# Loading i_gate and x in 4 KB runs, with word transposes of norm and gated input, GpSimd writing with a stride of two bf16

## Chip, cores, metric

One core of one Trainium2 chip. The metric is the device time of one execution in microseconds (us). A run counts as slow when it is over 1.5% above the fastest run of the same kernel; ratios use the other runs alone. The clock named here is the share of its full clock that PE was granted, as the trace records it. ACT is ScalarE, DVE is VectorE, POOL is GpSimd, PE is TensorE, SP issues the loads and stores. Medians and ratios below are of the runs named beside them.

## The reference, cut to what matters

Four sequences of 6336 tokens with 256 channels. A gated linear recurrence feeds a small gated unit:

```python
log_a = 8.0 * sigmoid(r_gate) * log(clip(sigmoid(a_param), 1e-6, 1 - 1e-6))
a_t = exp(log_a)
norm = sqrt(maximum(1.0 - a_t * a_t, 1e-6))
x_gated = norm * sigmoid(i_gate) * x
h = a_t[:, t] * h + x_gated[:, t]          # for each token t; y[:, t] = h
# then: gate = sigmoid(causal 5-tap convolution of y), out = (gate * (y @ w_val)) @ w_out
```

## The kernel before

Tokens pass in 28 chunks of up to 1024, split into 51 tiles of up to 512. The recurrence wants channels on the partitions, the loads bring tokens there, so PE transposes much. PSUM is the memory that PE writes its results to; a bank is a part of it. Each tile goes through these steps: load of r_gate, i_gate and x; `tanh` of both gates in one ACT instruction; `u2` = (tanh(i)+1)·x on DVE or POOL, as a string of letters says; `srT`, transpose of tanh(r); `exp`; `e` = a² on POOL; `sq` (square root on ACT, several chunks at once); `nT`, transpose of the norm back to tokens; `xg` = norm·u2 on DVE; `xT`, transpose of that to channels; `scan` on DVE; then `conv` (the convolution, PE), `tg` (tanh of it, ACT), `val` (y @ w_val, PE), `gv` (the gated value, DVE), `out` (times w_out, PE), `osb` (its copy out of PSUM, DVE or ACT) and `store`. Tiles in the traces are named by what holds them: `gp` is the result of conv, `bank` that of any transpose or of out.

The program is unrolled. A planner in the kernel (list scheduling) reads a table of costs and priorities, and emits every step in the order in which its model starts them. It also assigns PSUM banks that way. COST and PRIO do nothing else; OSB and U2 choose engines:

```python
OSB = "ADDDDDDDDDDDDADDD..."        # which engine copies each piece out of PSUM
U2 = "PDPDDDDDDPDPDPDPDDPDPPPP..."  # u2 of each tile on DVE (D, 15 tiles) or POOL (P, 36)
COST = dict(load=(0.05, 2.8), loadx=(0.02, 1.5), ..., u2P=(0.25, 3.15), u2D=(0.2, 1.55), ..., scan=(0.21, 2.14), ...,
            store=(0.05, 1.3))      # fixed part and part per tile or chunk, us
PRIO = dict(load=5.92, loadx=5.97, ...)
# ... make_plan: of all steps that could go next, take the one with the earliest start, ties by PRIO ...
order.sort(key=lambda o: o[0])
```

The parts that the change touches:

```python
# load: r_gate in 4 KB runs (a partition gets nj = 4 tokens in a row), i_gate and x in 1 KB runs
nc.sync.dma_start(ri[:, 0, 0:nw, 0:nj, :], rf[t0:t0 + nt, :].rearrange("(w p j) d -> p w j d", w=nw, j=nj))
nc.sync.dma_start(ri[:, 1, 0:nw, 0:nj, :]..., if_[t0:t0 + nt, :].rearrange("(k p) d -> p k d", p=P))
# u2
if eng == "DVE":
    nc.vector.scalar_tensor_tensor(out=u, in0=ti, scalar=1.0, in1=xt, op0=ALU.add, op1=ALU.mult)
else:
    nc.gpsimd.tensor_scalar(out=t1, in0=ti, scalar1=1.0, scalar2=1.0, op0=ALU.mult, op1=ALU.add)
    nc.gpsimd.tensor_tensor(out=u, in0=t1, in1=xt, op=ALU.mult)
# nT and xT: one bf16 transpose of 128x128 for each 128 tokens and 128 channels
nc.tensor.transpose(out=nT[:, j, h * P:(h + 1) * P], in_=nring[:, h, n0 + j * P:n0 + (j + 1) * P], identity=ident_b[:])
```

The output weight `wo` comes by a DMA from POOL's queue, and DVE halves it:

```python
nc.vector.tensor_scalar(out=wo[:], in0=wo[:], scalar1=0.5, scalar2=None, op0=ALU.mult)
```

Of the kernel before, what the change touches and what calls it, by code (L numbers as in the profile page):

```python
# [9 lines left out]
P = 128  # L10
WIN = 512
CHUNK = 1024
SUB = WIN // P
# [8 lines left out]
NU = 10  # L22
NY = 6
NIN = 2
NX = 3
NTR = 3
NTI = 5
# [7 lines left out]

U2 = "PDPDDDDDDPDPDPDPDDPDPPPPPPPPPPPPPPPDPPPPPPPDPPPPPPP"

COST = dict(load=(0.05, 2.8), loadx=(0.02, 1.5), tanh=(0.2, 1.7), u2P=(0.25, 3.15), u2D=(0.2, 1.55), srT=(0.05, 0.45), exp=(0.35, 0.86), e=(0.1, 1.8),
            sq=(0.3, 1.71), nT=(0.05, 0.47), xg=(0.1, 0.58), xT=(0.05, 0.45), scan=(0.21, 2.14), conv=(0.2, 1.1), tg=(0.19, 0.83),
            val=(0.02, 0.93), gv=(0.15, 1.07), out=(0.02, 0.47), osbD=(0.68, 0), osbA=(0.59, 0),  # L40
            store=(0.05, 1.3))
PRIO = dict(load=5.92, loadx=5.97, store=2.53, tanh=6, exp=2.8, sq=0.42, tg=-0.32, srT=-1.6, nT=0.31, xT=3.79,
            conv=5.3, val=4.34, out=2.99, e=5.93, u2=6, xg=4.55, scan=0.36, gv=-0.61, osb=-0.99)
TABLE, SEM, DMA_LAT = 1.3, 0.15, 2.2
# [1 line left out]
FP32 = mybir.dt.float32  # L46
BF16 = mybir.dt.bfloat16
ACT = mybir.ActivationFunctionType
ALU = mybir.AluOpType
# [60 lines left out]
def make_jobs(sh):  # L110
# [8 lines left out]
    def job(op, eng, f, deps, cost=None, bank=0):  # L119
        fix, per = COST[cost or op]  # L120
        jobs[op].append((eng, fix + per * f, [d for d in deps if d[1] >= 0], bank))
# [31 lines left out]
    for u, n in enumerate(UNITS):  # L153
        size = sum(sh.chunks[c][1] for c in range(ends[u] - n, ends[u])) / CHUNK
        fix, per = COST["sq"]
        jobs["sq"].append(("ACT", fix * len(sh.runs[u]) + per * size, [("e", 2 * ends[u] - 1)], 0))
# [57 lines left out]
def kernel(  # L214
# [11 lines left out]
    nc = tc.nc  # L226
    B, S, D = x.shape
# [3 lines left out]
    xf = x.rearrange("b s d -> (b s) d")  # L231
    rf = r_gate.rearrange("b s d -> (b s) d")
    if_ = i_gate.rearrange("b s d -> (b s) d")
    of = out.rearrange("b s d -> (b s) d")

    shape = Shape(B * S, S)
    tiles, chunks, chunk_of, pieces = shape.tiles, shape.chunks, shape.chunk_of, shape.pieces
    plan, banks = make_plan(shape)

    const = ctx.enter_context(tc.tile_pool(name="const", bufs=1))  # L240
    inp = ctx.enter_context(tc.tile_pool(name="inp", bufs=3))
    live = {}

    def load(c):
        t0, nt, g0, g1 = chunks[c]
        nw, nj = g1 - g0, nt // (g1 - g0) // P
        ri = inp.tile([P, 2, 2, SUB, D], FP32, name="ri", tag="ri", bufs=NIN)

        nc.sync.dma_start(ri[:, 0, 0:nw, 0:nj, :], rf[t0:t0 + nt, :].rearrange("(w p j) d -> p w j d", w=nw, j=nj))
        nc.sync.dma_start(ri[:, 1, 0:nw, 0:nj, :].rearrange("p w j d -> p (w j) d"),  # L250
                          if_[t0:t0 + nt, :].rearrange("(k p) d -> p k d", p=P))
        live["ri", c] = ri

    def loadx(c):
        t0, nt, g0, g1 = chunks[c]
        xt = inp.tile([P, 2 * SUB, D], FP32, name="xt", tag="xt", bufs=NX)
        nc.sync.dma_start(xt[:, 0:nt // P, :], xf[t0:t0 + nt, :].rearrange("(k p) d -> p k d", p=P))
        live["xt", c] = xt

    with tc.manual_schedule():  # L260
# [9 lines left out]
        ident_f = const.tile([P, P], FP32, name="ident_f")  # L270
        make_identity(nc, ident_f[:])
        ident_b = const.tile([P, P], BF16, name="ident_b")
# [15 lines left out]
        with tc.tile_pool(name="ps_setup", bufs=1, space=bass.MemoryType.PSUM) as ps_setup:  # L288
# [9 lines left out]
                                    op0=ALU.max, op1=ALU.min)  # L298
# [5 lines left out]
            for h in range(H):  # L304
                nc.tensor.transpose(out=wc_ps[:, h, :], in_=wrow[0:CONV_K, h * P:(h + 1) * P],
                                    identity=ident_f[0:CONV_K, 0:CONV_K])
# [8 lines left out]
        rings = ctx.enter_context(tc.tile_pool(name="rings", bufs=1))  # L315
        work = ctx.enter_context(tc.tile_pool(name="work", bufs=2))
        psum = ctx.enter_context(tc.tile_pool(name="psum", bufs=1, space=bass.MemoryType.PSUM))
        def bank(b, dtype):
            return psum.tile([P, WIN * 4 // mybir.dt.size(dtype)], dtype, name=f"bank{b}", tag=f"bank{b}", bufs=1)

        aring = rings.tile([P, H, NS * WIN], FP32, name="aring")
        ering = rings.tile([P, H, NE * WIN], FP32, name="ering")
        nring = ering[:].bitcast(BF16)
        tring = rings.tile([P, NTR + NTI, SUB, D], BF16, name="tring")
        uring = rings.tile([P, NU, SUB, D], BF16, name="uring")
        yring = rings.tile([P, H, NY * WIN], BF16, name="yring")

        def transposes(dst, srcs, h):
            col = 0
            for src, nj in srcs:  # L330
                for j in range(nj):
                    nc.tensor.transpose(out=dst[:, col:col + P], in_=src[:, j, h * P:(h + 1) * P],  # L332
                                        identity=ident_b[:])
                    col += P

        def op_load(g, eng):
            if ("load", g) not in before:
                load(g)
# [5 lines left out]
        def op_tanh(g, eng):  # L344
            nj = tiles[g][1] // P
            c = chunk_of[g]
            ri, w = live["ri", c], g - chunks[c][2]
            if g == chunks[c][3] - 1:
                del live["ri", c]
            r, i = g % NTR, NTR + g % NTI  # L350
            nc.scalar.activation(out=tring[:, r:i + 1:i - r, 0:nj, :], in_=ri[:, :, w, 0:nj, :], func=ACT.Tanh, scale=0.5)  # L351

        def op_u2(g, eng):
            nj = tiles[g][1] // P
            c = chunk_of[g]
            w = g - chunks[c][2]
            xt, ti = live["xt", c][:, w * nj:(w + 1) * nj, :], tring[:, NTR + g % NTI, 0:nj, :]
            u = uring[:, g % NU, 0:nj, :]
            if eng == "DVE":
                nc.vector.scalar_tensor_tensor(out=u, in0=ti, scalar=1.0, in1=xt, op0=ALU.add, op1=ALU.mult)  # L360
                return
            t1 = work.tile([P, SUB, D], FP32, name="t1", tag="t1", bufs=1)[:, 0:nj, :]
            nc.gpsimd.tensor_scalar(out=t1, in0=ti, scalar1=1.0, scalar2=1.0, op0=ALU.mult, op1=ALU.add)  # L363
            nc.gpsimd.tensor_tensor(out=u, in0=t1, in1=xt, op=ALU.mult)  # L364

        def op_srT(k, eng):
            c, h = k // 2, k % 2
            srT = bank(banks["srT", k], BF16)
            transposes(srT, [(tring[:, g % NTR], tiles[g][1] // P) for g in range(*chunks[c][2:])], h)
            live["srT", k] = srT  # L370

        def op_exp(k, eng):
# [17 lines left out]

        def op_nT(g, eng):
            c = chunk_of[g]
            n0, nt = shape.npos[c] + tiles[g][0] - chunks[c][0], tiles[g][1]
            nT = bank(banks["nT", g], BF16)[:].rearrange("p (j d) -> p j d", d=D)
            for h in range(H):
                for j in range(nt // P):
                    nc.tensor.transpose(out=nT[:, j, h * P:(h + 1) * P],  # L397
                                        in_=nring[:, h, n0 + j * P:n0 + (j + 1) * P], identity=ident_b[:])
            live["nT", g] = nT

        def op_xg(g, eng):
            nj = tiles[g][1] // P
            u = uring[:, g % NU, 0:nj, :]
            nc.vector.tensor_tensor(out=u, in0=live.pop(("nT", g))[:, 0:nj, :], in1=u, op=ALU.mult)  # L404

        def op_xT(k, eng):
            c, h = k // 2, k % 2
            xT = bank(banks["xT", k], BF16)
            transposes(xT, [(uring[:, g % NU], tiles[g][1] // P) for g in range(*chunks[c][2:])], h)
            live["xT", k] = xT  # L410

        def yend(c):
            return shape.ypos[c - 1] + chunks[c - 1][1] if c else 0
# [4 lines left out]
        def op_scan(k, eng):  # L418
            c, h = k // 2, k % 2
            t0, nt, g0, g1 = chunks[c]  # L420
            a0, y0 = shape.apos[c], shape.ypos[c]
            yp = yend(c) - 1
            xT = live.pop(("xT", k))
            for (c0, c1, fresh) in shape.segments(t0, nt):
                nc.vector.tensor_tensor_scan(  # L425
                    out=yring[:, h, y0 + c0:y0 + c1], data0=aring[:, h, a0 + c0:a0 + c1], data1=xT[:, c0:c1],
                    initial=0.0 if fresh else yring[:, h, yp:yp + 1], op0=ALU.mult, op1=ALU.add)
# [55 lines left out]
        def op_out(q, eng):  # L483
            g, i = pieces[q]
            gv = live["gv", g]
            ops = bank(banks["out", q], FP32)
            for e in range(2):
                for hk in range(H):
                    nc.tensor.matmul(out=ops[:, e * D:(e + 1) * D], lhsT=gv[:, 2 * i + e, hk, :], rhs=wo[:, hk, :],  # L489
                                     start=(hk == 0), stop=(hk == H - 1))  # L490
            live["ops", q] = ops
# [12 lines left out]
        def op_store(g, eng):  # L504
# [6 lines left out]
                           nT=op_nT, xg=op_xg, xT=op_xT, scan=op_scan, conv=op_conv, tg=op_tg, val=op_val, gv=op_gv,  # L511
                           out=op_out, osb=op_osb, store=op_store)
# [32 lines left out]
```

## Time and profile before

| before | |
|---|---|
| time, median of 2 | 320.17 us (317.40 and 322.94) |
| span of the profiled run, clock | 317.1 us, 0.973 |
| ACT busy / idle | 290.1 / 27.0 us |
| DVE, POOL busy | 270.4, 224.6 us |
| main DMA queue | 91.8% of the span, 291 us |

"Busy" is the sum of an engine's instructions in the span; idle is the span less that. The prediction below prints the lines of the busy table, the slices, the stretches and the waits.

### The profile page before, as it was taken

The numbers are of one execution on the slowest core, as the hardware profiler recorded it, in microseconds if no ns is written. First come the engines' busy times: TensorE is split into PE (matmuls) and PEld (weight loads), VectorE is DVE, ScalarE is ACT, GpSimd is POOL, SyncE is SP. The second block draws the span as 40 slices with busy tenths as digits, with TensorE's granted clock in tenths as the row PEclk, the third lists the DMA queues.
The fourth block names the chain that finished last, engine by engine and source line by source line (L and its number), as shares of the span: only waits on it lengthen the run. The fifth ranks groups of instructions, "written<-read, shape, count | busy, mean of one in ns | idle before, by whom it ended". The sixth has DMA issues, their size and how long they took to land.

```text
span 317.1 us, 7227 instructions
## 1 busy us (share of the span) xinstructions
PE 246.2 (78%) x2987; PEld 163.6 (52%) x2987; DVE 270.4 (85%) x269; ACT 290.1 (91%) x231; POOL 224.6 (71%) x140
## 2 busy tenths in 40 slices
PE   1262877687679768897989798959977997999994
PEld 1141745453546446564655375627644665655662
DVE  3125799999597998999999999997998999999892
ACT  6789999899969999999998999899989999998963
POOL 6329551869469536999989999999997289868000
PEclk9999999999759999999999999997999999999997
DMA  8999999999999999999999999996999994853334
GB/s 208 340 365 380 367 368 382 386 345 352 394 322 349 389 356 375 350 391 385 357 382 382 393 369 383 393 389 191 395 385 383 385 379 164 262 189 133 135 154 179
DMA packets 67327, 104.55 MB, mean 330 GB/s; under 512 B 3287, under 2 KB 54238, under 8 KB 67294
## 3 DMA queue, kind: packets, MB, share of 16 engines
q1 hardware_dynamic: 65904, 103.82, 91.8%
q0 software_dynamic: 1376, 0.26, 1.0%
q8 instruction: 23, 0.38, 0.5%
q14 instruction: 10, 0.08, 0.1%
q10 hardware_dynamic: 14, 0.01, 0.0%
HBM read 78.39 MB, written 25.95 MB: 329 GB/s over the span
## 4 chain that ended last, share of the span: by engine, by line
ACT 25%; DMA 23%; DVE 21%; PE 13%; issue 10%; POOL 4%; SPq 1%; DVEq 0%; ACTq 0%; POOLq 0%
DMA ri<-in_i_gate_dram 15%; DVE yring L425 9%; ACT tring L351 8%; DMA xt<-in_x_dram 6%; DVE gv L477 5%; ACT ering L388 5%; PE bank L489 4%; ACT tg L459 4%; ACT aring L376 4%; PE gp L451 3%; DVE osb L500 3%; PE bank L397 3%; POOL uring L364 2%; DMA ri<-in_r_gate_dram 2%; DVE uring L404 2%
## 5 line engine op out<-in xcount | busy, mean ns | idle before, releaser
L384 POOL TENSOR_TENSOR ering<-aring 128x1024 f32<-128x1024 f32 (+2 forms) x56 | 97.1, 1753 | 55.0 <-ACT aring L376 52.8
L425 DVE TENSOR_TENSOR_SCAN yring<-aring,yring,bank 128x1024 bf16<-128x1024 f32 (+5 forms) x54 | 110.1, 2052 | 0.7 <-PE bank L332 0.5
L351 ACT ACTIVATE tring<-ri 128x2048 bf16<-128x2048 f32 (+1 forms) x51 | 93.9, 1868 | 7.8 <-DMA ri<-in_i_gate_dram 7.7
L364 POOL TENSOR_TENSOR uring<-t,xt 128x1024 bf16<-128x1024 f32 (+1 forms) x36 | 83.6, 2323 | 9.9 <-DMA xt<-in_x_dram 7.3
L451 PE MATMUL gp<-yring,diag 64*64 64x512 bf16 (+14 forms) x1196 | 67.9, 350 | 6.7 <-ACT tg L459 4.6
L489 PE MATMUL bank<-wo,gv 128*128 128x256 bf16 x396 | 57.3, 279 | 18.5 <-DVE gv L477 8.2
L477 DVE SCALAR_TENSOR_TENSOR gv<-tg,val 128x1024 bf16<-128x1024 bf16 (+1 forms) x54 | 60.3, 1120 | 6.7 <-ACT tg L459 4.5
L376 ACT ACTIVATE aring<-bank,khf 128x1024 f32<-128x1024 bf16 (+2 forms) x56 | 59.6, 1111 | 3.3 <-PE bank L332 2.5
L459 ACT ACTIVATE tg<-gp 128x1024 bf16<-128x1024 f32 (+1 forms) x51 | 51.1, 1003 | 7.1 <-PE gp L451 6.8
L489 PEld LDWEIGHTS <-gv 128*128 128x128 bf16 x396 | 36.0, 99 | 37.9 <-issue 16.4
L467 PE MATMUL val<-yring,wv 128*128 128x512 bf16 (+1 forms) x204 | 51.5, 376 | 0.8 <-DVE gv L477 0.8
L500 DVE COPY osb<-bank 128x512 f32<-128x512 f32 x69 | 45.6, 679 | 3.8 <-PE bank L489 3.3
L451 PEld LDWEIGHTS <-diag 64*64 64x64 bf16 x1196 | 30.9, 108 | 33.0 <-issue 16.5
L388 ACT ACTIVATE ering<-ering,b 128x2048 bf16<-128x2048 f32 (+4 forms) x15 | 46.7, 3112 | 0.3
L332 PE MATMUL bank<-ident_b,tring 128*128 128x128 bf16 x396 | 31.3, 231 | 18.5 <-ACT tring L351 13.0
L397 PE MATMUL bank<-ident_b,ering 128*128 128x128 bf16 x396 | 32.9, 240 | 15.8 <-ACT ering L388 12.5
L404 DVE TENSOR_TENSOR uring<-bank,uring 128x1024 bf16<-128x1024 bf16 (+1 forms) x51 | 33.4, 669 | 11.8 <-PE bank L397 11.6
L363 POOL TENSOR_SCALAR t<-tring 128x1024 f32<-128x1024 bf16 (+1 forms) x36 | 40.1, 1115 | 2.6 <-ACT tring L351 1.2
L397 PEld LDWEIGHTS <-ering 128*128 128x128 bf16 x396 | 28.1, 108 | 23.3 <-ACT ering L388 15.5
L332 PEld LDWEIGHTS <-tring 128*128 128x128 bf16 x396 | 25.7, 103 | 27.7 <-ACT tring L351 15.1
L332 PE MATMUL bank<-ident_b,uring 128*128 128x128 bf16 x396 | 30.4, 226 | 3.3 <-DVE yring L425 1.8
L360 DVE SCALAR_TENSOR_TENSOR uring<-tring,xt 128x1024 bf16<-128x1024 bf16 x15 | 24.4, 1624 | 8.2 <-DMA xt<-in_x_dram 8.2
(32 smaller groups left out, 112.6 us busy)
## 6 DMA issues: line engine op xcount, KB each, us to landing
out_dram<-osb SPq DMA_DIRECT2D x48, 512.0 KB, 7.1
ri<-in_r_gate_dram SPq DMA_DIRECT2D x23, 1024.0 KB, 8.1
ri<-in_i_gate_dram SPq DMA_DIRECT2D x23, 1024.0 KB, 11.8
xt<-in_x_dram SPq DMA_DIRECT2D x23, 1024.0 KB, 10.7
ri<-in_r_gate_dram SPq DMA_DIRECT2D x2, 512.0 KB, 5.9
ri<-in_i_gate_dram SPq DMA_DIRECT2D x2, 512.0 KB, 8.1
xt<-in_x_dram SPq DMA_DIRECT2D x2, 512.0 KB, 8.1
ri<-in_r_gate_dram SPq DMA_DIRECT2D x3, 256.0 KB, 2.9
```

Of the source, the lines that this page charges most:

```text
L332: nc.tensor.transpose(out=dst[:, col:col + P], in_=src[:, j, h * P:(h + 1) * P], identity=ident_b[:])
L351: nc.scalar.activation(out=tring[:, r:i + 1:i - r, 0:nj, :], in_=ri[:, :, w, 0:nj, :], func=ACT.Tanh, scale=0.5)
L364: nc.gpsimd.tensor_tensor(out=u, in0=t1, in1=xt, op=ALU.mult)
L376: nc.scalar.activation(out=aring[:, h, a0:a0 + nt].rearrange("c (w p j) -> c w p j", p=P, j=nj), in_=live.pop(("srT", k))[:, 0:nt].rearran ...
L384: nc.gpsimd.tensor_tensor(out=ering[:, h, e0:e0 + nt], in0=a, in1=a, op=ALU.mult)
L388: nc.scalar.activation(out=nring[:, :, 2 * e0:2 * e0 + m], in_=ering[:, :, e0:e0 + m], func=ACT.Sqrt, scale=-0.25, bias=b025[:, 0:1])
L397: nc.tensor.transpose(out=nT[:, j, h * P:(h + 1) * P], in_=nring[:, h, n0 + j * P:n0 + (j + 1) * P], identity=ident_b[:])
L425: nc.vector.tensor_tensor_scan(out=yring[:, h, y0 + c0:y0 + c1], data0=aring[:, h, a0 + c0:a0 + c1], data1=xT[:, c0:c1], initial=0.0 if fr ...
L451: nc.tensor.matmul(out=gp[64 * h:64 * h + 64, m, c0:c1], lhsT=diag[rows, h, kk, rows], rhs=yring[rows, h, src:src + c1 - c0], start=(sh == 0),
L459: nc.scalar.activation(out=tg[:, :, 0:nt], in_=live.pop(("gp", g))[:, :, 0:nt], func=ACT.Tanh, scale=0.5)
L477: nc.vector.scalar_tensor_tensor(out=gv[:, 0:nj, hs, :].rearrange("c j h p -> c j (h p)"), in0=tg[:, hs, 0:nt].rearrange("c h (p j) -> c j ...
L489: nc.tensor.matmul(out=ops[:, e * D:(e + 1) * D], lhsT=gv[:, 2 * i + e, hk, :], rhs=wo[:, hk, :], start=(hk == 0), stop=(hk == H - 1))
```

## The change

Its intent: i_gate and x also in 4 KB runs, to make the DMA work lighter. Then a partition holds four tokens in a row, and two adjacent tokens of a channel have to end up side by side for the scan. So u2 is stored as pairs of bf16, and norm and gated input are transposed as 32-bit words, half as many transposes. GpSimd reads in order and writes every second bf16; DVE reads with a stride, writes in order, and needs two instructions for it.

```diff
-COST = dict(load=(0.05, 2.8), loadx=(0.02, 1.5), tanh=(0.2, 1.7), u2P=(0.25, 3.15), u2D=(0.2, 1.55), ...
-            store=(0.05, 1.3))
+COST = dict(load=(0.05, 2.72), loadx=(0.02, 1.37), tanh=(0.2, 1.7), u2P=(0.25, 3.4), u2D=(0.3, 1.75), ...
+            store=(0.05, 1.33))
...
+    def by_token(src, c):
+        t0, nt, g0, g1 = chunks[c]
+        return src[t0:t0 + nt, :].rearrange("(w p j) d -> p w j d", w=g1 - g0, p=P)
...
+        nc.sync.dma_start(ri[:, 0:nw, 0, 0:nj, :], by_token(rf, c))
+        nc.sync.dma_start(ri[:, 0:nw, 1, 0:nj, :], by_token(if_, c))
...
+        nc.sync.dma_start(xt[:, 0:nw, 0:nj, :], by_token(xf, c))
...
+                tk = ti.rearrange("p (w e) d -> p w d e", e=2)
+                for k in range(nj // 2):
+                    nc.vector.scalar_tensor_tensor(out=u[:, k], in0=tk[:, k], scalar=1.0, in1=xt[:, k], op0=ALU.add,
+                                                   op1=ALU.mult)
...
-            nc.gpsimd.tensor_tensor(out=u, in0=t1, in1=xt, op=ALU.mult)
+            nc.gpsimd.tensor_tensor(out=u.rearrange("p w d e -> p w e d"), in0=t1.rearrange("p (w e) d -> p w e d", e=2),
+                                    in1=xt.rearrange("p w d e -> p w e d"), op=ALU.mult)
...
+                    nc.tensor.transpose(out=nT[:, w * D + h * P:w * D + (h + 1) * P],
+                                        in_=ering[:, h, n0 + w:n0 + nw * P:nw], identity=ident_f[:])
...
+                    nc.tensor.transpose(out=xT[:, at + w:at + nw * P:nw],
+                                        in_=uring_w[:, g % NU, w * D + h * P:w * D + (h + 1) * P], identity=ident_f[:])
```

OSB, U2, PRIO and the sizes of the rings are left as they were.

More of the change, by code (lines that the diff above doesn't have):

```diff
@@ L36 @@
 U2 = "PDPDDDDDDPDPDPDPDDPDPPPPPPPPPPPPPPPDPPPPPPPDPPPPPPP"
-COST = dict(load=(0.05, 2.8), loadx=(0.02, 1.5), tanh=(0.2, 1.7), u2P=(0.25, 3.15), u2D=(0.2, 1.55), srT=(0.05, 0.45), exp=(0.35, 0.86), e=(0.1, 1.8),
+COST = dict(load=(0.05, 2.72), loadx=(0.02, 1.37), tanh=(0.2, 1.7), u2P=(0.25, 3.4), u2D=(0.3, 1.75), srT=(0.05, 0.45), exp=(0.35, 0.86), e=(0.1, 1.8),
             sq=(0.3, 1.71), nT=(0.05, 0.47), xg=(0.1, 0.58), xT=(0.05, 0.45), scan=(0.21, 2.14), conv=(0.2, 1.1), tg=(0.19, 0.83),
             val=(0.02, 0.93), gv=(0.15, 1.07), out=(0.02, 0.47), osbD=(0.68, 0), osbA=(0.59, 0),
-            store=(0.05, 1.3))
+            store=(0.05, 1.33))
 PRIO = dict(load=5.92, loadx=5.97, store=2.53, tanh=6, exp=2.8, sq=0.42, tg=-0.32, srT=-1.6, nT=0.31, xT=3.79,
@@ L247, in load @@
         ri = inp.tile([P, 2, 2, SUB, D], FP32, name="ri", tag="ri", bufs=NIN)
-        nc.sync.dma_start(ri[:, 0, 0:nw, 0:nj, :], rf[t0:t0 + nt, :].rearrange("(w p j) d -> p w j d", w=nw, j=nj))
-        nc.sync.dma_start(ri[:, 1, 0:nw, 0:nj, :].rearrange("p w j d -> p (w j) d"),
-                          if_[t0:t0 + nt, :].rearrange("(k p) d -> p k d", p=P))
+        nc.sync.dma_start(ri[:, 0:nw, 0, 0:nj, :], by_token(rf, c))
+        nc.sync.dma_start(ri[:, 0:nw, 1, 0:nj, :], by_token(if_, c))
         live["ri", c] = ri
@@ L255, in loadx @@
         t0, nt, g0, g1 = chunks[c]
-        xt = inp.tile([P, 2 * SUB, D], FP32, name="xt", tag="xt", bufs=NX)
-        nc.sync.dma_start(xt[:, 0:nt // P, :], xf[t0:t0 + nt, :].rearrange("(k p) d -> p k d", p=P))
+        nw, nj = g1 - g0, nt // (g1 - g0) // P
+        xt = inp.tile([P, 2, SUB, D], FP32, name="xt", tag="xt", bufs=NX)
+        nc.sync.dma_start(xt[:, 0:nw, 0:nj, :], by_token(xf, c))
         live["xt", c] = xt
@@ L317, with bank @@
         psum = ctx.enter_context(tc.tile_pool(name="psum", bufs=1, space=bass.MemoryType.PSUM))
-        def bank(b, dtype):
+        def bank(b, dtype=FP32):
             return psum.tile([P, WIN * 4 // mybir.dt.size(dtype)], dtype, name=f"bank{b}", tag=f"bank{b}", bufs=1)
@@ L324 @@
         tring = rings.tile([P, NTR + NTI, SUB, D], BF16, name="tring")
-        uring = rings.tile([P, NU, SUB, D], BF16, name="uring")
+        uring = rings.tile([P, NU, SUB * D], BF16, name="uring")
+        uring_w = uring[:].bitcast(FP32)
         yring = rings.tile([P, H, NY * WIN], BF16, name="yring")
-        def transposes(dst, srcs, h):
-            col = 0
-            for src, nj in srcs:
-                for j in range(nj):
-                    nc.tensor.transpose(out=dst[:, col:col + P], in_=src[:, j, h * P:(h + 1) * P],
-                                        identity=ident_b[:])
-                    col += P
         def op_load(g, eng):
@@ L350, in op_tanh @@
             r, i = g % NTR, NTR + g % NTI
-            nc.scalar.activation(out=tring[:, r:i + 1:i - r, 0:nj, :], in_=ri[:, :, w, 0:nj, :], func=ACT.Tanh, scale=0.5)
+            nc.scalar.activation(out=tring[:, r:i + 1:i - r, 0:nj, :], in_=ri[:, w, :, 0:nj, :], func=ACT.Tanh, scale=0.5)
         def op_u2(g, eng):
@@ L356, in op_u2 @@
             w = g - chunks[c][2]
-            xt, ti = live["xt", c][:, w * nj:(w + 1) * nj, :], tring[:, NTR + g % NTI, 0:nj, :]
-            u = uring[:, g % NU, 0:nj, :]
+            xt = live["xt", c][:, w, 0:nj, :].rearrange("p (w e) d -> p w d e", e=2)
+            ti = tring[:, NTR + g % NTI, 0:nj, :]
+            u = uring[:, g % NU, 0:nj * D].rearrange("p (w d e) -> p w d e", d=D, e=2)
             if eng == "DVE":
-                nc.vector.scalar_tensor_tensor(out=u, in0=ti, scalar=1.0, in1=xt, op0=ALU.add, op1=ALU.mult)
+                tk = ti.rearrange("p (w e) d -> p w d e", e=2)
+                for k in range(nj // 2):
+                    nc.vector.scalar_tensor_tensor(out=u[:, k], in0=tk[:, k], scalar=1.0, in1=xt[:, k], op0=ALU.add,
+                                                   op1=ALU.mult)
                 return
@@ L368, in op_srT @@
             srT = bank(banks["srT", k], BF16)
-            transposes(srT, [(tring[:, g % NTR], tiles[g][1] // P) for g in range(*chunks[c][2:])], h)
+            col = 0
+            for g in range(*chunks[c][2:]):
+                for j in range(tiles[g][1] // P):
+                    nc.tensor.transpose(out=srT[:, col:col + P], in_=tring[:, g % NTR, j, h * P:(h + 1) * P],
+                                        identity=ident_b[:])
+                    col += P
             live["srT", k] = srT
@@ L392, in op_nT @@
             c = chunk_of[g]
-            n0, nt = shape.npos[c] + tiles[g][0] - chunks[c][0], tiles[g][1]
-            nT = bank(banks["nT", g], BF16)[:].rearrange("p (j d) -> p j d", d=D)
+            n0, nw = (shape.npos[c] + tiles[g][0] - chunks[c][0]) // 2, tiles[g][1] // P // 2
+            nT = bank(banks["nT", g])
             for h in range(H):
-                for j in range(nt // P):
-                    nc.tensor.transpose(out=nT[:, j, h * P:(h + 1) * P],
-                                        in_=nring[:, h, n0 + j * P:n0 + (j + 1) * P], identity=ident_b[:])
+                for w in range(nw):
+                    nc.tensor.transpose(out=nT[:, w * D + h * P:w * D + (h + 1) * P],
+                                        in_=ering[:, h, n0 + w:n0 + nw * P:nw], identity=ident_f[:])
             live["nT", g] = nT
         def op_xg(g, eng):
-            nj = tiles[g][1] // P
-            u = uring[:, g % NU, 0:nj, :]
-            nc.vector.tensor_tensor(out=u, in0=live.pop(("nT", g))[:, 0:nj, :], in1=u, op=ALU.mult)
+            n = tiles[g][1] // P * D
+            u = uring[:, g % NU, 0:n]
+            nc.vector.tensor_tensor(out=u, in0=live.pop(("nT", g))[:].bitcast(BF16)[:, 0:n], in1=u, op=ALU.mult)
         def op_xT(k, eng):
             c, h = k // 2, k % 2
-            xT = bank(banks["xT", k], BF16)
-            transposes(xT, [(uring[:, g % NU], tiles[g][1] // P) for g in range(*chunks[c][2:])], h)
+            xT = bank(banks["xT", k])
+            at = 0
+            for g in range(*chunks[c][2:]):
+                nw = tiles[g][1] // P // 2
+                for w in range(nw):
+                    nc.tensor.transpose(out=xT[:, at + w:at + nw * P:nw],
+                                        in_=uring_w[:, g % NU, w * D + h * P:w * D + (h + 1) * P], identity=ident_f[:])
+                at += nw * P
             live["xT", k] = xT
@@ L422, in op_scan @@
             yp = yend(c) - 1
-            xT = live.pop(("xT", k))
+            xT = live.pop(("xT", k))[:].bitcast(BF16)
             for (c0, c1, fresh) in shape.segments(t0, nt):
@@ L485, in op_out @@
             gv = live["gv", g]
-            ops = bank(banks["out", q], FP32)
+            ops = bank(banks["out", q])
             for e in range(2):
```

## The prediction

> **What bounds the kernel now.** I read the page's busy line and its 40 slices first, to see whether one engine is the limit.
>
> ```profile
> PE 246.2 (78%) x2987; PEld 163.6 (52%) x2987; DVE 270.4 (85%) x269; ACT 290.1 (91%) x231; POOL 224.6 (71%) x140
> ACT  6789999899969999999998999899989999998963
> POOL 6329551869469536999989999999997289868000
> DMA  8999999999999999999999999996999994853334
> ```
>
> ACT (ScalarE) has the most work, and the DMA engines read 9 in nearly every slice until about slice 33 of 40. DVE and, in slices 17 to 30, POOL (GpSimd) are nearly full too. So there is no single bound; it must be read stage by stage. The view of stretches (columns: stretch, its length, then busy us and instructions of PE, PEld, DVE, ACT, POOL, then clock, DMA share, GB/s) gives it:
>
> ```profile
> 20.00:120.00 100.00, 69.84 (x760) 47.93 (x761) 81.94 (x76) 93.85 (x64) 61.08 (x30) 0.95 1.04 366
> 120.00:200.00 80.00, 70.08 (x932) 46.36 (x935) 77.07 (x74) 78.54 (x58) 75.24 (x44) 1.00 1.06 377
> 200.00:260.00 60.00, 51.19 (x666) 34.97 (x659) 56.71 (x51) 56.46 (x45) 50.15 (x29) 0.97 1.00 362
> 260.00:318.00 58.00, 48.98 (x592) 30.53 (x590) 49.26 (x50) 46.84 (x52) 28.16 (x21) 0.96 0.48 175
> ```
>
> ACT's idle time is the length less its busy time: 6.15 us in 20 to 120, 1.46 in 120 to 200, 3.54 in 200 to 260, 11.16 in the end, where DMA is at half load and the last chunks drain through dependent steps. The waits tell who makes ACT idle (total us, times, longest):
>
> ```profile
> ACT tring L351 <- DMA ri<-in_i_gate_dram: 7.7, 7, 2.0
> ACT tg L459 <- PE gp L451: 6.8, 8, 2.0
> ACT aring L376 <- PE bank L332: 2.5, 4, 1.5
> ```
>
> ```profile
> DVE uring L404 <- PE bank L397: 11.6, 15, 4.1
> DVE uring L360 <- DMA xt<-in_x_dram: 8.2, 3, 3.9
> ```
>
> ```profile
> POOL ering L384 <- ACT aring L376: 52.8, 16, 7.3
> POOL uring L364 <- DMA xt<-in_x_dram: 7.3, 4, 3.4
> ```
>
> Loads cost the three engines 7.7, 8.2 and 7.3 us directly, and the chain that ended last agrees:
>
> ```profile
> ACT 25%; DMA 23%; DVE 21%; PE 13%; issue 10%; POOL 4%; SPq 1%; DVEq 0%; ACTq 0%; POOLq 0%
> ```
>
> My reading: up to about 120 us the loads pace the kernel with ACT close behind; from 120 to 200 ACT, DVE, POOL and DMA are all at 94% or more; later ACT and DVE lead; the last 55 us are latency.
>
> **What the Trainium skill says.** "DMA: Bandwidth & Descriptors", section "Why small descriptors are slow (HBM only)", gives about 3 cycles of overhead per packet beside one cycle per 32 bytes. By that, an estimate is 4 x (32+3) = 140 cycles for four 1 KB packets against 131 for one of 4 KB, 6% less. The trace says more: I averaged its individual packet records: 50688 of 1024 B took 49.7 ns each, 12288 of 4096 B 165.8 ns. Four small ones are 198.9 ns, so 17% less for the same bytes. I use the trace. "GPSIMD Engine Reference", section "Performance pitfalls for Q7 kernels": reads whose step is over 8 bytes cost about half as much again per element. That is why this change lets GpSimd read in order. About writes with a step of 4 bytes that section has no row; nothing in this trace shows one. "TensorE: Matmul & The Clock Gate", section "Weight-path perf modes", says the fast weight load does not work for FP32. The trace of before has only two tiny setup transposes in f32 of similar kind, but they agree in direction (ns min/median/max):
>
> ```profile
> L305 PEld LDWEIGHTS wc_ps<-ident_f,wrow x2: 178/198/219, 3.5 to 3.6; 5*128 5x128 f32 x2
> L397 PEld LDWEIGHTS <-ering x396: 95/98/151, 13.9 to 299.5; 128*128 128x128 bf16 x198
> ```
>
> "PSUM — Partial Sum Buffer", section "Specifications (TRN2)", warns that non-contiguous output patterns slow matmuls; the new transposes of the gated input write f32 words with a step of two. No trace row shows that here.
>
> **The change part by part.**
>
> (1) Loads. r_gate is already loaded in 4 KB runs per partition; i_gate and x now are too. All 50688 packets of 1 KB become about 12288 of 4 KB and 768 of 2 KB (the three half tiles). Packet time: 50688 x 49.7 ns = 2519 us, against 12288 x 165.8 + 768 x 105.7 (the 2048 B packets of now) = 2118 us; over 16 engines 157.4 becomes 132.4, so 25 us less DMA work out of 291 (91.8% of the span on the main queue). The new rows of the kernel's own cost table are more timid: per 1024 tokens loads go from 5.65+3.02 to 5.49+2.76 us and the store from 1.35 to 1.38, about 0.4 us times 24.75 chunks, 10 us. Between 10 and 25 us of transfer work goes. What of it lies on the path is bounded by what starves the engines: ACT's idle time between 20 and 260 us is 6.15+1.46+3.54 = 11 us, and only part of that is due to loads. I take 5 us in the first stage, 0.5 in the second, 1.5 in the third: 7 us.
>
> (2) Norm and gated-input transposes. 396 + 396 bf16 transposes become 198 + 198 of f32 words, so PE falls from 2987 to 2591 instructions. A pair (load and matmul) now comes about every 105 to 120 ns (24 in a row took 2.84 us). If an f32 weight load takes about 200 ns instead of 98 and half as many are made, the load side is equal: 8 x 0.1 against 4 x 0.2 us per tile. A gain of 10% or a loss of 50% of some 85 us of spread-out work is possible, but PE has slack in most stages (0.65 to 0.88 busy, and that modelled). I book 0 us, with a risk below.
>
> (3) DVE's part of u2 (15 tiles): one instruction of 1024 elements becomes two of 512. The fixed part of a DVE instruction comes from two forms of one line, L477: 1208 ns at 1024 elements and 418 at 256, so 1.03 ns per element and 155 ns fixed. 15 x 155 ns = 2.3 us; the cost table's 1.75 to 2.05 would be 4.5 us. Most of these tiles come before 120 us, where DVE is 82% busy, so little of it shows: I book 0.5 us.
>
> (4) GpSimd's part (33 full and 3 half tiles): the multiply took 2419 ns on a full tile, in order on all sides. It now reads in order and writes with a step of two bf16. The cost table goes from 3.40 to 3.65 us for both steps, 0.25 us more; 33 x 0.25 + 3 x 0.125 = 8.6 us of POOL work. From about 140 to 230 us POOL is full; nine pairs of scans in 133.9 to 229.0 us are 10.6 us per chunk, so some 8.5 chunks with nearly two such tiles each pass there: 8.5 x 2 x 0.25 = 4 us if all of it shows. I book 3 us, as POOL may get its inputs earlier than now.
>
> (5) Everything on ACT, the scans, the convolution, value, output and stores are the same in number and shape. The multiply by norm reads and writes the same contiguous bf16 as before, 669 ns. The order of instructions shifts with the cost table; I give it 0 us, plus or minus 2.
>
> Sum: -7 + 0 + 0.5 + 3 = -3.5 us from about 319 us (the mean of the three times seen: 322.94, 317.4 and the profiled 318.93 is 319.8). That is 315.5 to 316; I say 315.5.
>
> **The rivals.** A: the loads get the full 25 us lighter and GpSimd's stepped write is free. Then ACT alone sets the pace: 290 us busy, plus the first 20 us' idle 5.6, plus some 9 at the end, 304 to 308 us. For it: DMA is full for 33 slices and three engines wait on loads. Against: ACT has only 11 us of idle time to give between 20 and 260. B: GpSimd becomes the bound. If the stepped write costs half as much again on the multiply, 36 tiles gain about 1.2 us each, some 42 us; POOL would rise from 225 to 267 us and its full stage would lengthen by about 8.5 x 2 x 1.2 = 20 us, to 330 or more. For it: POOL's slices 17 to 30 are full, and x buffers are released by POOL (the queue waits 17.0 us for it). Against: the cost table of the change expects only 0.25. C: the transfer was hidden anyway and nothing moves: DMA keeps a backlog of three or four transfers (10 us from issue to landing for 1 MB), yet ACT is 98% busy from 120 to 200; then 318 to 321. D: f32 transposes take two or three times as long each as bf16 ones; the multiply by norm, which waits 11.6 us for them already, waits some 10 more, and part of that reaches the end: 322 to 326.
>
> **Range and chances.** The middle is -1%. A has about a quarter, C and the small loss or gain around it more than half, B and D together about an eighth. The range 306 to 326 holds A's upper half through D. Faster by over 2% (under about 313) 0.28, within 2% 0.60, slower 0.12.
>
> **What the profile after would show.** Step 1 is right if packets fall to about 29,000, the main queue's share to 81 to 88%, and the waits of ACT, DVE and POOL on loads to under half of 23 us. Step 2: PE with some 2591 instructions, a word transpose's weight load near 200 ns, DVE's wait for the norm transposes not above 12 us. Step 3: two instructions of 512 of some 680 to 900 ns each. Step 4: POOL's multiply at 2.4 to 2.7 us; above 3 us is rival B. ACT's busy time must stay at 290 us. The prediction fails most likely by POOL's write being much dearer, or by DMA relief turning into more than 7 us because POOL and DVE run less often into each other.

## The result, and the profile after

348.2 us, median of 2 (346.4 and 350.0), against 320.17: ratio 1.0889, 95% interval 1.0656 to 1.1121. Ratios and intervals are from fast runs that were measured in the same rounds, so not quite the ratio of the medians. The change is 28 us slower.

The page of the changed kernel: engines, slices, packets, main queue.

```profile
PE 258.1 (74%) x2561; PEld 167.0 (48%) x2591; DVE 281.9 (81%) x284; ACT 291.2 (84%) x231; POOL 221.0 (63%) x140
...
ACT  5829999969967798889999699798989999978443
...
DMA  8966997988899928999999989998799672303433
...
DMA packets 29692, 104.50 MB, mean 300 GB/s; under 512 B 3287, under 2 KB 3550, under 8 KB 29662
...
q1 hardware_dynamic: 28272, 103.82, 77.7%
```

The DMA work fell as meant: 77.7% of 348.2 us is 270.5 us, 20.6 less than before. POOL did not get more work, ACT's is the same, DVE has 11.5 us more. The span grew by 31.1 us, and ACT's idle time by 30.0 (348.2 - 291.2 = 57.0 against 27.0). So nearly all of the loss is waiting on the fullest engine, spread over all stages. The stretches of the changed kernel (same columns as in the prediction):

```profile
20.00:120.00 100.00, 69.76 (x581) 45.66 (x590) 80.12 (x78) 83.07 (x57) 52.23 (x28) 0.88 0.87 331
120.00:200.00 80.00, 64.96 (x683) 41.21 (x684) 75.05 (x72) 71.54 (x50) 69.05 (x39) 0.98 0.90 348
200.00:260.00 60.00, 50.31 (x528) 33.56 (x534) 52.21 (x48) 54.87 (x42) 51.46 (x30) 0.91 0.91 347
```

ACT has 83.07 us of work in 20 to 120 where it had 93.85, and 71.54 where it had 78.54. DMA no longer fills its time (0.87 for 1.04). Nothing took the place of the old bound: in the first two stretches every engine is less busy. Who makes ACT, DVE and POOL wait, in the changed kernel (total us, times, longest):

```profile
ACT tg L474 <- PE gp L466: 20.4, 12, 6.4
ACT tg L474 <- DVE gv L492: 10.0, 5, 2.8
ACT tring L350 <- DMA ri<-in_i_gate_dram: 7.1, 7, 1.4
```

```profile
DVE uring L413 <- PE bank L406: 26.0, 17, 11.1
DVE wo L318 <- DMA wo<-in_moe_w_out_dram: 13.9, 1, 13.9
DVE gv L492 <- PE val L482: 8.6, 7, 2.4
```

```profile
POOL uring L367 <- DMA xt<-in_x_dram: 0.4, 1, 0.4
```

Waits on x loads are all but gone. In their place ACT waits for the convolution (20.4 us, 6.8 before) and for gv (10.0, none before), DVE for the norm transposes (26.0, 11.6 before), and once, 13.9 us long, for the output weight. The convolution and gv are untouched by the change, and PE's matmuls for the norm transposes grew only from 32.9 to 36.6 us in all. That points to the order in which the steps stand. DVE's first entries in the two traces (start, duration), first before:

```profile
13.49 0.29 DVE L313 TENSOR_SCALAR wo<-wo 128x512 bf16<-128x512 bf16 x1 [7.14 <-DMA wo<-in_moe_w_out_dram]
14.60 0.42 DVE L404 TENSOR_TENSOR uring<-bank,uring 128x512 bf16<-128x512 bf16 x1 [0.82 <-PE bank L397]
```

and after:

```profile
20.25 0.29 DVE L318 TENSOR_SCALAR wo<-wo 128x512 bf16<-128x512 bf16 x1 [13.89 <-DMA wo<-in_moe_w_out_dram]
20.45 1.30 DVE L362 SCALAR_TENSOR_TENSOR uring<-tring,xt 128x512 bf16<-128x512 bf16 x2
21.67 0.42 DVE L413 TENSOR_TENSOR uring<-bank,uring 128x512 bf16<-128x512 bf16 x1
```

In the trace after, DVE runs nothing in the 13.89 us before 20.25: all that it has to do stood behind the halving of a weight that is first needed some microseconds later. Before, that wait cost almost nothing, as the next step waited for PE until 14.60 anyway. After, that step (the first multiply by norm) starts 7.1 us later, and so does the first scan (22.66 for 15.59 us).

Last, u2 on both engines (ns min/median/max), before and then after:

```profile
L364 POOL TENSOR_TENSOR uring<-t,xt x36: 1264/2366/3320, 11.3 to 290.2; 128x1024 bf16<-128x1024 f32 x33, 128x512 bf16<-128x512 f32 x3
L360 DVE SCALAR_TENSOR_TENSOR uring<-tring,xt x15: 1198/1381/2480, 24.3 to 265.8; 128x1024 bf16<-128x1024 bf16 x15
```

```profile
L367 POOL TENSOR_TENSOR uring<-t,xt x36: 1272/2365/2906, 9.7 to 307.6; 128x1024 bf16<-128x1024 f32 x33, 128x512 bf16<-128x512 f32 x3
L362 DVE SCALAR_TENSOR_TENSOR uring<-tring,xt x30: 679/702/2868, 20.5 to 271.7; 128x512 bf16<-128x512 bf16 x30
```

POOL's stepped write cost nothing here: medians 2366 and 2365 ns. DVE's halves run from 679 to 2868 ns; thirty of them keep DVE busy for 37.0 us (mean 1272 ns) where 15 whole ones took 24.4 (mean 1624).

### The profile page after: what moved, and what is told of

It is laid out like the page before. It is cut to its first block, busy times and chain, and to the rows that moved or that the text cites.

```text
span 348.2 us, 6453 instructions
## 1 busy us (share of the span) xinstructions
PE 258.1 (74%) x2561; PEld 167.0 (48%) x2591; DVE 281.9 (81%) x284; ACT 291.2 (84%) x231; POOL 221.0 (63%) x140
## 2 busy tenths in 40 slices
DMA packets 29692, 104.50 MB, mean 300 GB/s; under 512 B 3287, under 2 KB 3550, under 8 KB 29662
## 3 DMA queue, kind: packets, MB, share of 16 engines
q1 hardware_dynamic: 28272, 103.82, 77.7%
## 4 chain that ended last, share of the span: by engine, by line
DVE 30%; POOL 20%; PE 19%; issue 18%; ACT 7%; DMA 6%; DVEq 0%; POOLq 0%; ACTq 0%
DVE yring L440 11%; POOL uring L367 10%; DVE gv L492 8%; PE bank L504 6%; DVE uring L362 5%; POOL ering L393 5%; PE gp L466 5%; DMA wo<-in_moe_w_out_dram 4%; POOL t L366 4%; DVE osb L515 4%; PE val L482 3%; PE bank L406 3%; ACT tring L350 2%; DMA xt<-in_x_dram 2%; DVE uring L413 2%
## 5 line engine op out<-in xcount | busy, mean ns | idle before, releaser
L393 POOL TENSOR_TENSOR ering<-aring 128x1024 f32<-128x1024 f32 (+2 forms) x56 | 95.4, 1723 | 72.9 <-ACT aring L385 68.0
L466 PE MATMUL gp<-yring,diag 64*64 64x512 bf16 (+14 forms) x1196 | 72.4, 367 | 8.0 <-ACT tg L474 5.4
L504 PE MATMUL bank<-wo,gv 128*128 128x256 bf16 x396 | 58.9, 285 | 25.4 <-DVE gv L492 18.5
L474 ACT ACTIVATE tg<-gp 128x1024 bf16<-128x1024 f32 (+1 forms) x51 | 51.0, 999 | 30.5 <-PE gp L466 20.4
L504 PEld LDWEIGHTS <-gv 128*128 128x128 bf16 x396 | 37.4, 101 | 46.2 <-DVE gv L492 26.4
L482 PE MATMUL val<-yring,wv 128*128 128x512 bf16 (+1 forms) x174 | 48.4, 385 | 4.2 <-DVE gv L492 2.3
L466 PEld LDWEIGHTS <-diag 64*64 64x64 bf16 x1196 | 32.8, 114 | 38.5 <-issue 25.0
L406 PE MATMUL bank<-ident_f,ering 128*128 128x128 f32 x198 | 36.6, 328 | 16.9 <-ACT ering L397 14.1
L366 POOL TENSOR_SCALAR t<-tring 128x1024 f32<-128x1024 bf16 (+1 forms) x36 | 37.9, 1053 | 16.1 <-ACT tring L350 14.8
L376 PE MATMUL bank<-ident_b,tring 128*128 128x128 bf16 x396 | 31.5, 230 | 18.7 <-ACT tring L350 12.4
L406 PEld LDWEIGHTS bank<-ident_f,ering 128*128 128x128 f32 x198 | 29.8, 210 | 25.0 <-ACT ering L397 11.7
L422 PE MATMUL bank<-ident_f,uring 128*128 128x128 f32 x198 | 32.3, 294 | 10.2 <-DVE uring L413 8.4
L362 DVE SCALAR_TENSOR_TENSOR uring<-tring,xt 128x512 bf16<-128x512 bf16 x30 | 37.0, 1272 | 0.6 <-ACT tring L350 0.6
```

Of the source, the lines that this page charges most:

```text
L376: nc.tensor.transpose(out=srT[:, col:col + P], in_=tring[:, g % NTR, j, h * P:(h + 1) * P], identity=ident_b[:])
L393: nc.gpsimd.tensor_tensor(out=ering[:, h, e0:e0 + nt], in0=a, in1=a, op=ALU.mult)
L406: nc.tensor.transpose(out=nT[:, w * D + h * P:w * D + (h + 1) * P], in_=ering[:, h, n0 + w:n0 + nw * P:nw], identity=ident_f[:])
L466: nc.tensor.matmul(out=gp[64 * h:64 * h + 64, m, c0:c1], lhsT=diag[rows, h, kk, rows], rhs=yring[rows, h, src:src + c1 - c0], start=(sh == 0),
L482: nc.tensor.matmul(out=val[:, m, 0:nt], lhsT=wv[:, hk, m * P:(m + 1) * P], rhs=yring[:, hk, y0:y0 + nt], start=(hk == 0), stop=(hk == H - 1))
L504: nc.tensor.matmul(out=ops[:, e * D:(e + 1) * D], lhsT=gv[:, 2 * i + e, hk, :], rhs=wo[:, hk, :], start=(hk == 0), stop=(hk == H - 1))
```

## The experiments

Theories at the start: **order** (the new cost table makes the planner issue a worse order), **late start** (the output weight), **data path** (the new instructions themselves: DVE's halves, the word transposes). Medians are of 4 runs (e11: 6), slow ones included, with runs of the kernel before on the same chip in each batch. Batches ran on different chips, so versions of different batches (e1 to e4, e5 to e8, e9 to e11, e12) are best compared by their ratios.

| run | median us | ratio to before (95%) |
|---|---|---|
| the change | 348.2 | 1.0889 (1.0656 to 1.1121) |
| e1 new data path, old order | 332.05 (325.18 to 334.94) | none, three of four runs slow |
| e2 old data path, new order | 344.55 | 1.0794 (1.0711 to 1.0876) |
| e3 change, weight halved late | 343.23 | 1.0770 (1.0697 to 1.0843) |
| e4 = e1 + e3 | 326.46 | 1.0255 (1.0184 to 1.0326) |
| e5 before, scan's cost +1% | 334.77 | 1.0430 (1.0357 to 1.0504) |
| e6 = e4, plain u2 on DVE | 319.33 | 0.9960 (0.9895 to 1.0024) |
| e7 = e4, 1 KB loads | 327.61 | 1.0213 (1.0114 to 1.0312) |
| e8 = e4, bf16 transposes | 325.01 | 1.0122 (1.0059 to 1.0185) |
| e9 before, x load's cost +2% | 327.62 | 1.0213 (1.0146 to 1.0280) |
| e10 = e4, u2 in two plain halves | 328.09 | 1.0244 (1.0167 to 1.0321) |
| e11 change, settings searched anew | 326.12 | 1.0181 (1.0119 to 1.0243) |
| e12 = e4, POOL reads with the stride | 358.45 | 1.1228 (1.1156 to 1.1300) |

e6, e7, e8 and e10 give a wrong result, as their layouts no longer fit; durations and dependencies are those of the right program.

### e1 to e4: order against data path, and the late start

e1 is the change with the cost table of before, e2 is before with the table of the change, so only the order differs, with the PSUM banks that the planner hands out along with it:

```diff
-COST = dict(load=(0.05, 2.72), loadx=(0.02, 1.37), ..., u2P=(0.25, 3.4), u2D=(0.3, 1.75), ..., store=(0.05, 1.33))
+COST = dict(load=(0.05, 2.8), loadx=(0.02, 1.5), ..., u2P=(0.25, 3.15), u2D=(0.2, 1.55), ..., store=(0.05, 1.3))
```

> The changed data path with the cost table of before, so that instructions and PSUM banks are issued in the order of before. Theory 1 (the order, re-made from the new cost table, is what costs most): the span falls from 348 to about 325 us, with the 7 us late start left in it. Theory 2 (the new data path itself costs: u2 on DVE 12.6 us dearer, word transposes slower): it stays at 340 us or more.

> The kernel before with only the cost table of the change, so the old data path in the new order. Theory 1: 335 to 345 us, slower than before by 5 to 8%. Theory 2: within 2% of before, 315 to 325 us.

e3 moves the halving of the weight; e4 does that and has the old table:

```diff
-        nc.vector.tensor_scalar(out=wo[:], in0=wo[:], scalar1=0.5, scalar2=None, op0=ALU.mult)
...
             live["gv", g] = gv
+            if g == 0:
+                nc.vector.tensor_scalar(out=wo[:], in0=wo[:], scalar1=0.5, scalar2=None, op0=ALU.mult)
```

> The changed kernel, with the scaling of the output weight moved on DVE from the setup to just after the first gated value. Theory of the late start (DVE stands 13.9 us on the landing of that weight, twice as long as before, and everything behind it starts 7 us later): the span falls by about 7 us, to 341. If the late start is absorbed later, it falls by less than 3 us.

> Both: old order and the weight scaled late. If order and late start are the two causes and add up, about 318 us, within 2% of before; if the new data path costs by itself, 330 us or more.

e2 settles the main point. Not one instruction of it differs in kind, size or number from before, and it takes 344.55 us: the re-made plan alone costs 8%. That is the order and the PSUM banks together (make_plan, run off the chip, changes 178 of 262 bank assignments); no run parts the two. Its ACT is busy 290.4 us in a span of 343.8, so idle 53.4, 26.4 more than before. The waits on ACT in e2:

```profile
ACT tring L351 <- DMA ri<-in_i_gate_dram: 18.0, 9, 3.3
ACT tg L459 <- PE gp L451: 12.4, 9, 2.3
ACT tg L459 <- DVE gv L477: 10.0, 5, 2.8
```

The waits of tg on the convolution and on gv are those of the change, the first smaller (12.4 for 20.4 us); the 10.0 us on gv, which before has not at all, is the same to the digit, in e3 too. All five of these stand in the drain, from 321 to 335 us in e2. With the old data path the i_gate loads hurt too, 18.0 us for 7.7. The loss builds up all along: of the 54 gv instructions, e2 starts the first 2.2 us later than before, the 17th 11.0 and the last 26.7.

e3 is faster than the change by 5.0 us by medians and 3.8 by ratios. The intervals overlap, as the change has only two runs, so the times alone do not prove it. The two traces do for these two executions, as the order in them is the same: the first gv starts at 26.32 us in the change and at 19.82 in e3, the last at 343.22 and 335.85. The lag of 6.5 us is 7.4 at the end, so the late start was not absorbed. With the weight late in both, the old order is worth 343.23 - 326.46 = 16.8 us. e1 misses its number: its runs spread from 325 to 335, three of them over 1.5% above the fastest, so the median is no measure. In its profiled run DVE waited 12.2 us for the weight. Its fastest run, 325.18, is like e4's 325.12; that the weight came in time there is a guess, as that run was not profiled. e4 is 2.5% slower than before, between the two expectations, so the data path has a cost of its own.

### e5 and e9: is it the new numbers, or any new order?

```diff
-... scan=(0.21, 2.14) ...        # e5
+... scan=(0.21, 2.1614) ...
-... loadx=(0.02, 1.5) ...        # e9
+... loadx=(0.02, 1.53) ...
```

> The kernel before, data path and all, with one number of its cost table moved by 1%: the scan's slope from 2.14 to 2.1614. No instruction gets longer or shorter; only the order that the planner makes from the table changes. Theory 1a (the settings of before are tuned to one exact order, and any other order that the same planner makes loses time): slower than before by 2 to 5%, 326 to 335 us. Theory 1b (it is the particular numbers of the new table that mislead the planner): within 1.5% of before.

> Control to e5: the kernel before with another number of its cost table moved, the x load's slope by 2% (1.5 to 1.53). The order differs in 332 places against 474 in e5, but the planner's own end is only 2.3 us later (320.7 against 318.4; e5 328.6; the change 333.0). If the length of the plan decides (theory 1c): within 2% of before, 319 to 324 us. If any other order loses by some contention that the planner does not know (1a): 328 us or more.

One per cent on one number of the table costs 4.3%; nothing in the data path is touched. So it does not take the new numbers to lose time. The settings of before fit their one order, and all three re-made ones (e2, e5, e9) are worse. The planner itself sees a part of it. From make_plan run off the chip: the last end in its own list, each by its own table, and the places where an engine's list differs from before (of 1005):

| table of | planned end us | places changed | measured ratio |
|---|---|---|---|
| before | 318.4 | 0 | 1 |
| e9 | 320.7 | 332 | 1.0213 |
| e5 | 328.6 | 474 | 1.0430 |
| the change (e2's order) | 333.0 | 622 | 1.0794 |

The rank is right, and each loses 1.1 to 3.4% of the time of before more than planned (e2: 4.6% planned, 7.9% measured). e9 came out at 327.62, between its two expectations (0.7% planned, 2.1% measured): the length of the plan is one part, and something that the planner does not know adds to it. What that is stays open, and so does which of the moved steps cost most.

### e6, e10, e7, e8: what the data path costs in the old order

```diff
# e6 (e10 the same, in two instructions of 512 elements)
-                    nc.vector.scalar_tensor_tensor(out=u[:, k], in0=tk[:, k], scalar=1.0, in1=xt[:, k], ...)
+                nc.vector.scalar_tensor_tensor(out=uring[:, g % NU, 0:nj * D], in0=ti.rearrange("p j d -> p (j d)"), ...)
# e7
-        nc.sync.dma_start(ri[:, 0:nw, 1, 0:nj, :], by_token(if_, c))
+        nc.sync.dma_start(ri[:, 1, 0:nw, 0:nj, :]..., if_[t0:t0 + nt, :].rearrange("(k p) d -> p k d", p=P))   # and x so
# e8: the two transposes as in the kernel before
```

> Old order and late weight as in e4, but DVE's part of u2 as one plain instruction of 1024 elements, read and written in order (wrong result on purpose: the layout is then not the one that the word transposes want). If the split on DVE makes most of the remaining 7 us: DVE busy falls by about 12 us and the time from 326 to 320 or 321. If the word transposes make it: 325 or more.

> As e6 (old order, weight late, DVE reads and writes in order, wrong result on purpose), but cut into two instructions of 512 elements as the change has it. If the cut itself costs, because the second half stands behind the GpSimd instruction that began meanwhile: 325 to 328 us like e4, DVE busy about 282 us. If it was the strided reading: 319 to 321 us like e6.

> Old order and late weight as in e4, but i_gate and x loaded in 1 KB runs as before (wrong result on purpose: the tokens then lie on other partitions). It shows what the 4 KB loads alone are worth in this order. If the loads pace it: 330 to 336 us. If they were hidden: within 2 us of 326.

> Old order and late weight as in e4, but norm and gated input transposed by bf16 as before, twice as many instructions (wrong result on purpose: the two tokens of a word are not paired). If word transposes are dearer and on the path: 322 us or less, and DVE's wait for the norm transposes falls from 18.7 to about 12 us. If they cost nothing: 326.

e6 takes back all of the 2.5% (0.996, even with before), and e10, whose instructions read in order but are cut in two, loses it again (1.0244). So it is the cut, not the strided reading. The fixed part of 155 ns explains 15 x 0.155 = 2.3 us, but DVE's work fell by 282.4 - 269.7 = 12.7 us from e4 to e6. The other 10 us are more waiting. The instruction groups of e6, then e10 (ns min/median/max), whose instructions read the same data in the same order:

```profile
L359 DVE SCALAR_TENSOR_TENSOR uring<-tring,xt x15: 1202/1226/2946, 22.3 to 267.1; 128x1024 bf16<-128x1024 bf16 x15
L362 DVE SCALAR_TENSOR_TENSOR uring<-tring,xt x30: 665/882/2845, 22.9 to 272.5; 128x512 bf16<-128x512 bf16 x30
```

A stretch of before, where x landed for both engines at once:

```profile
82.80 1.23 DVE L360 SCALAR_TENSOR_TENSOR uring<-tring,xt 128x1024 bf16<-128x1024 bf16 x1 [3.40 <-DMA xt<-in_x_dram]
...
82.94 3.32 POOL L364 TENSOR_TENSOR uring<-t,xt 128x1024 bf16<-128x1024 f32 x1 [3.38 <-DMA xt<-in_x_dram]
```

and of e4:

```profile
82.20 3.48 DVE L361 SCALAR_TENSOR_TENSOR uring<-tring,xt 128x512 bf16<-128x512 bf16 x2 [1.82 <-DMA xt<-in_x_dram]
82.34 2.78 POOL L366 TENSOR_TENSOR uring<-t,xt 128x1024 bf16<-128x1024 f32 x1 [2.90 <-DMA xt<-in_x_dram]
```

Before, DVE began first and took its 1.23 us; POOL's multiply, 2.37 us as a rule, took 3.32, so it stood behind DVE. In e4 POOL is held for the first half only (2.78 us), and then DVE's second half is held for the whole of POOL's instruction: 3.48 us for two halves that take 0.69 us each where POOL is idle (eight of the thirty in that trace, 689 to 696 ns). The row merges the two; singly, the second half took 2.86 us, began 0.48 us after POOL's multiply and ended 0.55 us after its end. The Trainium skill has the rule: "SBUF — State Buffer", section "Who interferes with whom", says that a DVE instruction with two SBUF inputs contends with a GpSimd instruction that reads SBUF, and "Issue order, not op shape, decides who blocks". This trace agrees. Cutting the instruction handed the turn to POOL in the middle. I had read the page but used it for nothing.

e7: without the 4 KB loads e4 does not get measurably slower: 1.2 us slower by medians (327.61 for 326.46), 1.3 us faster by ratios, and the intervals leave room for some 4 us either way. The packets' saving is there. The main queue in e4, then in e7:

```profile
q1 hardware_dynamic: 28272, 103.82, 84.7%
q1 hardware_dynamic: 65904, 103.82, 90.3%
```

That is 274 us of 323.3 against 293 of 324.7. But the engines hardly get their data sooner by it: the waits of ACT, DVE and POOL on loads are 13.8 us in e4 and 15.4 in e7. e6 fits: with 4 KB loads and no cut it is no faster than before, though the word transposes are in it too.

e8: bf16 transposes in place of words bring 1.0122 for 1.0255, so between 1.5 us (medians) and 4 us (ratios); the intervals just touch, so the size is uncertain. It was measured with the cut in place; in e6, without the cut, word transposes and 4 KB loads together cost nothing measurable, so these parts need not add. DVE's wait for the norm transposes is 17.7 us for 18.7, not the fall to 12 that I expected.

### e11: does a fitting order take the gain?

OSB, U2, PRIO and the planner's table were searched anew with a replay of fixed orders, on costs from these traces; the data path is the change's with the weight late.

```diff
-U2 = "PDPDDDDDDPDPDPDPDDPDPPPPPPPPPPPPPPPDPPPPPPPDPPPPPPP"
+U2 = "DPDPDDDDPPDDPDPDPPPPPPPPPPPPPPPPPPPDPPPPPPPPPPPPPPP"
# and other OSB, PRIO, COST
```

> The new data path with the weight scaled late and the planner's settings searched anew by a fixed-order replay with costs from these traces (word transposes, and DVE's halves waiting for GpSimd's current instruction). The replay has it 5.8 us ahead of e4's order, so 320 to 322 us, no better than before. If the 4 KB loads have a gain that only a fitting order can take: 316 us or less.

326.12 us, 1.0181: no better than e4 within the noise, worse than expected by 4 to 6 us, so the replay's 5.8 us did not come through. No version here beats the kernel before. That a better order for the new data path exists is not ruled out.

### e12: the side of GpSimd's stride

```diff
-            nc.gpsimd.tensor_tensor(out=u.rearrange("p w d e -> p w e d"), in0=t1.rearrange("p (w e) d -> p w e d", e=2),
-                                    in1=xt.rearrange("p w d e -> p w e d"), op=ALU.mult)
+            nc.gpsimd.tensor_tensor(out=u, in0=t1.rearrange("p (w e) d -> p w d e", e=2), in1=xt, op=ALU.mult)
```

> As e4 (old order, weight late, right result), but GpSimd's multiply the other way round: it writes in order and reads both inputs with a step of 256 elements. This is what the change avoids. If the side of the stride matters as the skill's GpSimd page says for reads over 8 bytes: the multiply goes from 2.42 us to 3 us or more, POOL from 223 to 243 us or more, and the time over 330 us. If GpSimd does not mind either way: 2.42 us and 326 us.

The multiply in e12 (ns min/median/max):

```profile
L366 POOL TENSOR_TENSOR uring<-t,xt x36: 1938/3823/4169, 9.4 to 330.2; 128x1024 bf16<-128x1024 f32 x33, 128x512 bf16<-128x512 f32 x3
```

3823 ns for 2370 in e4, 61% more, POOL busy 272.7 us for 223.5, and 358.45 us in all. So writing with the stride and reading in order was the right side, worth 32 us against the other; it is not what made the change slow.

## Why the prediction was wrong, step by step

**The step that failed is (5)**: "The order of instructions shifts with the cost table; I give it 0 us, plus or minus 2." It is worth 16.8 us in the new data path (e3 to e4) and 25 us in the old (e2). I had seen that the table was edited and that U2, OSB and PRIO were not. I took a re-made order for noise around the old one; each of the three that were run on the old data path was a loss, of 2 to 8%. By medians the way from the change over e3 and e4 to before is 5.0 + 16.8 + 7.3 = 29 us: late start, order, and the data path with the weight late. Why the new order is worse, step by step, stays open.

**A term was missing**: the late start. It is worth 4 to 5 us by the times of e3, 7 by the traces. My reading of before listed no wait for the weight, though DVE's waits have it (7.1 us), because it cost nothing there. Why it landed so late is not settled: 14.5 us from issue in the change, 14.6 in e3, 12.9 in e1, but 5.0 to 8.0 in the other six kernels with 4 KB loads and 7.7 to 8.9 in those with 1 KB. So it came in three of the nine kernels with 4 KB loads and in none of the five with 1 KB; the 4 KB loads do not force it.

**Step (3) was mis-sized**: 0.5 us booked, 7.1 us by medians (e4 to e6) and about 9 by ratios (2.95% of 320). The 155 ns per cut is right (halves alone take 0.69 us, 1.38 together, for 1.21). The blocking by POOL is what I left out, 10 of the 12.7 us of DVE work.

**Step (1) was right about the DMA and wrong about the time.** Packets 29692 (29,000 foretold), work down by 20.6 us (10 to 25), waits on loads under half of 23 us (7.1 + 0.4); the queue's share, 77.7%, fell below the 81 to 88% foretold because the span grew. But of the 7 us of gain none could be measured (e7). The engines' waits on loads were not made by the bytes in the way I took it: rival C had this right for this term, "the transfer was hidden anyway". The waits of SP, which issues loads and stores, suggest a reason that no run tests; before, then e4:

```profile
SPq L507 <- DVE osb L500: 116.2, 35, 7.0
SPq L523 <- DVE osb L516: 152.6, 41, 8.1
```

In e4 SP stands 152.6 us on DVE's output copies (116.2 before) and 39.9 on tanh (35.0) before it issues the next transfer. If these set when a load starts, landing faster frees little. From this view the prediction took only the 17.0 us on POOL.

**Step (2) was about right**: 198 + 198 transposes and 2591 weight loads, a price of 1.5 to 4 us for the 0 that I booked; its sign, a wait for the norm transposes of at most 12 us, failed. **Step (4) was wrong on the safe side**: 0 for 3 us; rival B is refuted. Rival D named the right wait, DVE on the norm transposes, 26.0 us in the change, but that wait by itself tells little: in e6, no slower than before, it is 23.7 us.

Two slips in its sums change nothing: the cost table's store row is for 512 tokens, so loads and store save 0.36 us a chunk by it, 9 us and not 10; and 3.5 off the mean of 319.8 is 316.3.

The chances: "slower" had 0.12, from B and D; the cause that came was in none of my rivals. The granted clock is lower in the slow orders (0.942, e2 0.929), yet e3 at 0.959 takes 343 us and e4 at the same clock 326, so the loss does not need a lower clock.

## What to carry to other kernels

When a kernel's order is made by a planner with tuned settings, a change of its cost table is a change of the kernel: run the old data path with the new table, and the new one with the old table, before you judge the data path. Before cutting an instruction of DVE that reads two SBUF tensors, look at what GpSimd runs at that time, for here a half that takes 0.69 us alone took up to 2.9 us behind one. And before you count work saved on transfers, look at what the queue waits for before it issues them; here 20 us less DMA work gained nothing measurable.

## What the Trainium skill lacked or had wrong

- "GPSIMD Engine Reference", pitfalls: no row for stepped writes. A write with a step of two bf16 cost nothing (median 2365 ns for 2366). Its row for stepped reads holds, and is low for two inputs: 61% more here (3823 for 2370 ns), for about half.
- "SBUF — State Buffer": its contention rule holds; it does not spell out that cutting the instruction lets GpSimd in between (two halves 3.48 us, alone 1.38).
- "DMA: Bandwidth & Descriptors": its overhead of 3 cycles per packet gives an estimate of 6% for 1 KB against 4 KB packets, about 8% with the 32 bytes of metadata per descriptor that the same section names; the records show 17% before (198.9 for 165.8 ns), with 169.4 ns per 4 KB packet after. It has no figure for how late a small transfer of POOL's queue lands beside large ones (14.5 us for 7.7).
- "TensorE: Matmul & The Clock Gate" and "PSUM — Partial Sum Buffer": neither has the price of a 32-bit word transpose. Here the matmul's median is 273 ns with an output step of two words and 284 with none, so the step did not show as far as modelled matmul ends can tell; the weight load is 141 ns read in order and 209 read with a step of two words, for 98 in bf16.
